# Strassen once more on a third of P4, two convolution steps on ScalarE and GpSimd, and S3 and S4 in other buffers

## The chip, the cores and the metric

One core of a Trainium2 chip. The time is the device time in microseconds (us) of one execution, the median of several. Engines: PE (TensorE), DVE (VectorE), ACT (ScalarE), POOL (GpSimd); SP only issues DMAs.

## The reference, cut

`x` is (8, 4096, 192) and `weight` (8, 7), float32; `w_in` is (192, 2048) and `w_out` (2048, 192).

```python
w = softmax(weight)                       # over the 7 taps, for each of 8 heads
x_unf = x_pad[:, idx, :].reshape(B, S, K, H, group)
y = np.einsum('hk,bskhg->bshg', w, x_unf) # causal convolution over the sequence
h = y.reshape(B * S, D) @ w_in
g = h * np.clip(h + 3.0, 0.0, 6.0) / 6.0
return g @ w_out
```

## The kernel before, in words

The 32768 tokens are cut into 32 blocks of 1024. Block 0 goes another way while the weights are prepared; blocks 1 to 31 run the same program: `first_layer(i)`, then `second_layer(i)`. Every engine works its instructions off in the order in which the code issues them, and the code writes that order out by hand.

**Convolution.** `conv_jobs` (L855) makes seven steps over y, 128 x 1536 numbers each: step 0 is a multiplication on ACT, steps 1 to 6 are multiply-and-add instructions on DVE that read x and y from SBUF. For block i + 2 the first three are placed in `second_layer(i)`; the other four lie in the next `first_layer` (ahead of chunk 0 and behind chunks 1, 5 and 9). `split_high` and `split_rest` then cut y into three parts `y_own`, one instruction on ACT and two on DVE, and `swap_parts` copies them, with the two halves of the partitions exchanged, into `y_other`: six DMAs on SP's queue.

**First layer.** There are 16 chunks. For chunk n, `begin(n)` issues 12 matmuls into one of four PSUM slots of two banks and a multiplication by 4097 on ACT; `end(n)` issues 6 more, then `relu` on ACT and `gate` on DVE (L306), which write g to SBUF and free the slot. PE runs two chunks ahead of the gates. Chunks 0 to 7 read `y_own` and chunks 8 to 15 `y_other`. A slot is taken from the head of `free_slots` and put back at its end.

**Second layer.** g is 2 x 2 parts A11, A12, A21, A22 (8 pieces of 128 x 512 each), and so is w_out. Strassen's scheme makes seven products P1 to P7 of the sums S1 to S4 and T1 to T4 (table `prod`). A product is 512 tokens by 96 columns in three column pieces q = 0, 1, 2 of 32. PE works with four column streams j = 0 to 3 side by side, each 32 columns wide. `plain` puts eight 512-column matmuls (2 units each) on a stream; `small` puts four 256-column matmuls (1 unit each) of a second Strassen step on one. Before, the third piece (q = 2) of P1 and of P5 is made by such a second step on stream 3, seven small products each in place of one plain one; the parts they need are `small_sums` (L565): of A11 on POOL into tile `s1` during the first layer, of S1 on DVE into A22's place. Each stream holds 82 units. `do(t, fn)` places work for the other engines at unit t; all events are then sorted by t and issued.

**Sums.** S3 = A11 - A21 has a buffer of its own: three of the four pairs of pieces are made on POOL during the first layer, the last on DVE. S1 = A21 + A22 lies in A21's place: two pairs by accumulating DMAs that POOL issues (L552), two by DVE. S2 (in A11's place) and S4 (in A12's) are made by DVE in the second layer, in halves of 128 x 2048.

**End of the block.** DVE adds the products, transposes them, and SP stores them. Two `finish` jobs for the second half of the columns are carried over into the next block's first layer, where they stand ahead of chunk 0's gate on DVE. The second layer uses three of the four PSUM slots, so the next `begin(0)` finds a free one at once.

Of the kernel before, what the change touches and what calls it, by code (L numbers as in the profile page):

```python
# [25 lines left out]
def kernel(  # L26
# [93 lines left out]
    w_s = cst.tile([P, 2, 4, NP // 2, QS], F32, name="w_s")  # L120
# [154 lines left out]
    S2, S1, S4 = A11, A21, A12  # L275
# [101 lines left out]
    def out_direct(i, work):  # L377

        parts = [(k, q) for k in range(G) for q in range(G * NQ)]
        for r in range(0, len(parts), 4):  # L380
# [14 lines left out]
            if r == 0:  # L395
                for u in work:
                    u()
# [3 lines left out]
            for j, (k, q) in enumerate(parts[r : r + 4]):  # L401
                store_rows(i, k, q, xt, j)

    def g_sums(engine, which, slots, width):

        forms = {
            3: (S3, A11, A21, ALU.subtract),
            2: (S2, S1, A11, ALU.subtract), 4: (S3, A12, S2, ALU.subtract),
        }
        for n in which:  # L410
            o, a, b, op = forms[n]
            for p in slots[::width]:
                r = slice(p, p + width)
                engine.tensor_tensor(out=o[:, r], in0=a[:, r], in1=b[:, r], op=op)  # L414
# [7 lines left out]
    def product(bank, j, n, q, ks=every, **tokens):  # L422
        x, w = prod[n]
        return mm(bank, j, S3 if n == 7 else x, w, q, ks, True, True, **tokens)
# [65 lines left out]
    y_own, y_other, pools, s1 = [], [None], [], []  # L490

    def swap_parts():
        y_other[0] = pools[0].tile([P, 3, K3, N], F32, name="y_other", tag="other")
        for n in range(3):
            swap(y_other[0][:, n], y_own[n])


    def first_layer(i, jobs):
# [6 lines left out]
        def mms(n, part, start=False, stop=False):  # L505
            group, c = divmod(n, NP)
            for s in range(K3):
                for k in range(2):
# [3 lines left out]
                        rhs=r32(y_other[0][r, part, s] if group else y_own[part][r, s]),  # L512
# [23 lines left out]
        for n in range(count):  # L536
# [7 lines left out]
            if n == 1:  # L544
                s1.append(ot.tile([P, NP, N], F32, name="s1", tag="shared")[:])
            if n < NP and n % 2:
                small_sums(s1[-1], A11, (1, 2, 3, 4), nc.gpsimd, every[n - 1 : n + 1])
            if n > NP and n % 2:
                pair = slice(n - NP - 1, n - NP + 1)
                g_sums(nc.gpsimd if n + 1 < count else nc.vector, (3,), range(NP)[pair], 2)  # L550
                if n + 3 < count:
                    nc.gpsimd.dma_start(out=S1[:, pair], in_=A22[:, pair], accum_op=ALU.add)  # L552
        for pair in (slice(NP - 2, NP), slice(NP - 4, NP - 2)):
# [21 lines left out]
    def small_weights(to, w):  # L575
# [4 lines left out]
        t1, t2, t3, t4 = (to[:, n] for n in range(4))  # L580
# [3 lines left out]
    def second_layer(i, between):  # L584
        last = i + 1 == NB
        ours = [free_slots.pop(0) for _ in range(3)]
        d, e, b, x_, a, c = (psum[:, 2 * n + k] for n in ours for k in range(2))
        s5 = A22
# [4 lines left out]
        B, C, V = (bank[rows(3)] for bank in (x_, d, b))  # L593
        A, E = e[rows(3)], a[rows(3)]
        first, second, third = rows(0), rows(1), rows(2)
        late = {}
# [17 lines left out]
        def plain(j, bank, n, q, chunks, start=False):  # L614
            x, w = prod[n]
            x = S3 if x is None else x
# [6 lines left out]
        def small(n, m_, out, start=False):  # L623

            x, w = prod[n]
            sums, ws = (s1[-1], w_s[:, 0]) if n == 1 else (s5, w_s[:, 1])
            x11, x12, x21, x22 = four_parts(x)
            z1, z2, z3, z4 = four_parts(sums)
# [3 lines left out]
            t1, t2, t3, t4 = (ws[:, k] for k in range(4))  # L632
            xm, wm = {
                1: (x11, b11), 2: (x12, b21), 3: (z4, b22), 4: (x22, t4),
                5: (z1, t1), 6: (z2, t2), 7: (z3, t3),
            }[m_]
            for u in range(NP // 2):
                put(3, 1, lambda u=u: matmul(
                    3, out[:, lo], wm[:, u], xm[:, u], start and u == 0
                ))  # L640

        def tiles():
            new_results()
            late.update(zip(("p7", "p5", "u3"), (results[0][m, n] for n in range(3))))

        for q in range(NQ):
            plain(q, d, 4, q, every, True)
            before = (1, 6, NP)[q]
            plain(q, c, 7, q, every[:before], True)
            plain(q, e, 1, 2, range(5 + q, 6 + q))  # L650
            do(clock[q], copy, out=e[rows(q + 1)] if q < 2 else p1[third], in_=e[rows(q)])
            plain(q, c, 7, q, every[before:])
            plain(q, a, 2, q, every[:6], True)
            plain(q, b, 6, q, every)
            plain(q, a, 2, q, every[6:])
            plain(q, b, 3, q, every)

        def level_two(n, p, chunks, order):
            chunks, first_fill = list(chunks), [True]

            def fill(k):
                plain(3, b, n, 2, [chunks.pop(0) for _ in range(k)], first_fill.pop() if first_fill else False)

            steps = {
                1: lambda: copy(out=B[:, lo], in_=A[:, lo]),
                2: lambda: copy(out=p()[first, lo], in_=A[:, lo]),
                6: lambda: copy(out=C[:, lo], in_=B[:, lo]),
                5: lambda: copy(out=p()[second, lo], in_=E[:, lo]),
                7: lambda: add(p()[second, hi], C[:, lo], p()[second, lo]),
                3: lambda: add(p()[second, lo], B[:, lo], p()[second, lo]),  # L670
                4: lambda: copy(out=p()[first, hi], in_=C[:, lo]),
            }
            to = {1: A, 2: A, 6: B, 5: E, 7: C, 3: B, 4: C}
            for step in order.split():
                if step[0] == "x":
                    fill(int(step[1]))
                else:
# [275 lines left out]
```

## Time and profile before

| | us |
|---|---|
| median of 3 runs | 2231.11 (2230.29 to 2231.27) |
| profiled execution, its own time | 2230.5 |
| its span, first to last instruction | 2228.4 |
| PE busy | 2219.4 (100%) |
| DVE busy | 1872.5 (84%) |
| ACT busy | 1390.0 (62%) |
| POOL busy | 827.7 (37%) |

The granted TensorE clock was 1.0 throughout. The page counts an instruction as busy from its recorded start to its end, so time in which it is held up inside counts too. In a timeline, a line gives the start in us, the length, engine, source line, operation, output and input, shapes, and in brackets how long the engine was idle before and what released it. L numbers are lines of the kernel before; PEld is the loading of weights, which runs ahead of the matmuls.

What the groups of the page give for the operations that the change touches (mean of one):

| operation | engine | ns |
|---|---|---|
| convolution step, 128 x 1536 (L861) | DVE | 1807 |
| multiplication of convolution step 0 (L859) | ACT | 1575 |
| S3 difference of a pair, 128 x 1024 (L414) | POOL | 3040 |
| the same | DVE | 1339 |
| small sum of a pair, 128 x 256 (L573) | POOL | 755 to 1095 |
| small sum of all pieces, 128 x 1024 (L573) | DVE | 1223 |
| half of S2 or S4, 128 x 2048 (L414) | DVE | 2284 |
| gate, 128 x 1024 (L306) | DVE | 1219 |
| addition, 96 x 512 (L458) | DVE | 668 to 689 |
| addition, 32 x 256 (L458) | DVE | 427 |

### The profile page before, as it was taken

To read this page: it belongs to the slowest core of one execution; us is meant where nothing else is said; L and a number is where in the kernel's file an instruction comes from. 1 tells how busy PE (TensorE), PEld (TensorE's weight loads), DVE (VectorE), ACT (ScalarE), POOL (GpSimd) and SP (SyncE) were. 2 spreads that over 40 slices of the span, in tenths; PEclk is the share of its full clock that TensorE was granted. 3 is DMA by queue.
4 is the path that set the end of the run, shared out by engine and by line. 5 is a ranking of instruction groups with operands and counts; after the bars stand their busy time and mean duration, and the time that the engine had idled before them with its cause. 6 is when DMAs were issued, how large, how long until landed. Compare 5 with 4: busy or idle time off the path is not lost.

```text
span 2228.4 us, 50173 instructions
## 1 busy us (share of the span) xinstructions
PE 2219.4 (100%) x21432; PEld 1528.0 (69%) x21432; DVE 1872.5 (84%) x1636; ACT 1390.0 (62%) x1676; POOL 827.7 (37%) x689
## 2 busy tenths in 40 slices
PE   9999999999999999999999999999999999999998
PEld 5467776677766777766777667776667776677765
DVE  8888888888888888888888888888888888888876
ACT  7467665576655676555776556665567665577653
POOL 2444432344422444223443234442244432344322
PEclk9999999999999999999999999999999999999999
DMA  6344224443244342344422443323444234443232
GB/s 157 69 84 86 48 59 91 84 84 62 54 82 91 78 80 46 71 91 84 84 50 56 91 89 79 71 48 79 91 81 85 48 61 91 84 84 59 52 72 34
DMA packets 254063, 166.57 MB, mean 75 GB/s; under 512 B 208528, under 2 KB 213648, under 8 KB 253840
## 3 DMA queue, kind: packets, MB, share of 16 engines
q1 hardware_dynamic: 235416, 129.53, 28.4%
q0 software_dynamic: 17184, 33.57, 8.7%
q8 instruction: 168, 2.75, 0.5%
q14 instruction: 55, 0.45, 0.1%
q10 hardware_dynamic: 1240, 0.27, 0.1%
HBM read 31.72 MB, written 25.17 MB: 26 GB/s over the span
## 4 chain that ended last, share of the span: by engine, by line
PE 100%; DVE 0%; issue 0%; ACT 0%; DVEq 0%
PE psum L609 49%; PE psum L510 46%; PE psum L296 2%; PE psum L341 2%; PE psum L755 0%; PE psum L763 0%; DVE results L458 0%; DVE results L464 0%; ACT results L709 0%; DVE zeros L111 0%; DVEq L464 0%; DVE x L96 0%; DVE half L233 0%; DVE bias_e L150 0%; DVE bias_e L149 0%
## 5 line engine op out<-in xcount | busy, mean ns | idle before, releaser
L609 PE MATMUL psum<-g,w_out 128*32 128x512 f32 (+1 forms) x6696 | 967.3, 553 | 0.0
L306 DVE SCALAR_TENSOR_TENSOR g<-g,psum 128x1024 f32<-128x1024 f32 (+1 forms) x528 | 618.1, 1186 | 228.2 <-ACT g L302 223.9
L573 POOL TENSOR_TENSOR s<-g 128x256 f32<-128x256 f32 x248 | 271.6, 1095 | 1232.3 <-DVE g L306 1232.3
L302 ACT ACTIVATE g<-psum,half 128x1024 f32<-128x1024 f32 (+1 forms) x528 | 565.1, 1089 | 0.8
L609 PEld LDWEIGHTS psum<-g,w_out 128*32 128x32 f32 x6696 | 368.9, 110 | 247.3 <-issue 127.4
L521 ACT ACTIVATE psum<-psum 128x1024 f32<-128x1024 f32 x496 | 500.2, 1008 | 57.7 <-PE psum L510 55.9
L510 PE MATMUL psum<-y,w_in 64*128 64x512 f32 x4464 | 521.7, 388 | 0.0
L510 PE MATMUL psum<-y_other,w_in 64*128 64x512 f32 x4464 | 517.0, 386 | 0.0
L510 PEld LDWEIGHTS psum<-y,w_in 64*128 64x128 f32 x4464 | 413.3, 184 | 116.1 <-issue 26.0
L510 PEld LDWEIGHTS psum<-y_other,w_in 64*128 64x128 f32 x4464 | 415.7, 184 | 91.0 <-ACT psum L521 5.1
L609 PE MATMUL psum<-s,w_out 128*32 128x512 f32 (+1 forms) x3224 | 465.3, 576 | 0.0
L861 DVE SCALAR_TENSOR_TENSOR y<-x,c_sb,y 128x1536 f32<-128x1536 f32 x186 | 336.1, 1807 | 1.3
L414 POOL TENSOR_TENSOR s<-g 128x1024 f32<-128x1024 f32 x93 | 282.7, 3040 | 30.2 <-DVE g L306 30.2
L609 PE MATMUL psum<-g,w_s 128*32 128x256 f32 x1240 | 282.8, 379 | 0.0
L609 PEld LDWEIGHTS psum<-s,w_out 128*32 128x32 f32 x3224 | 151.7, 110 | 81.7 <-issue 50.0
L609 PEld LDWEIGHTS psum<-g,w_s 128*32 128x32 f32 x1240 | 136.4, 110 | 68.4
L414 DVE TENSOR_TENSOR s<-g 128x2048 f32<-128x2048 f32 (+1 forms) x93 | 180.6, 1969 | 1.1
L609 PE MATMUL psum<-s,w_s 128*32 128x256 f32 x744 | 170.7, 379 | 0.0
L573 DVE TENSOR_TENSOR g<-g 128x1024 f32<-128x1024 f32 x124 | 151.7, 1223 | 5.2
L414 DVE TENSOR_TENSOR g<-g 128x2048 f32<-128x2048 f32 x62 | 139.1, 2284 | 0.0
L606 ACT COPY psum<-psum 32x512 f32<-32x512 f32 x93 | 51.3, 551 | 131.9 <-PE psum L609 131.9
L458 DVE TENSOR_TENSOR results<-psum,results 32x256 f32<-32x256 f32 (+1 forms) x125 | 68.0, 544 | 47.7 <-issue 46.3
(82 smaller groups left out, 1270.7 us busy)
## 6 DMA issues: line engine op xcount, KB each, us to landing
y_other<-y SPq DMA_DIRECT2D x186, 384.0 KB, 5.1
g<-g POOLq DMA_DIRECT2D x62, 512.0 KB, 5.0
out_dram<-results SPq DMA_DIRECT2D x378, 64.0 KB, 2.0
x<-in_x_dram SPq DMA_DIRECT2D x53, 388.5 KB, 7.7
stage<-in_moe_w_in_dram SPq DMA_DIRECT2D x16, 192.0 KB, 4.6
stage<-in_moe_w_out_dram SPq DMA_DIRECT2D x8, 384.0 KB, 5.6
x<-in_x_dram SPq DMA_DIRECT2D x7, 384.0 KB, 8.3
x<-in_x_dram POOLq DMA_DIRECT2D x2, 388.5 KB, 6.7
```

What stands on the lines that cost most here:

```text
L296: nc.tensor.matmul(out=psum[:, b], lhsT=w[r], rhs=src, start=start, stop=stop, skip_group_check=onto,)
L302: nc.scalar.activation(r6, h, ACT.Relu, bias=half[:], scale=1.0 / 6.0)
L306: nc.vector.scalar_tensor_tensor(out=g_, in0=g_, scalar=1.0, in1=h, op0=ALU.min, op1=ALU.mult)
L341: lambda p=p: nc.tensor.matmul(out=bank[j * QS : (j + 1) * QS, tokens], lhsT=w_out[:, p, w, cols], rhs=x[:, p, tokens], start=(first and p ...
L414: engine.tensor_tensor(out=o[:, r], in0=a[:, r], in1=b[:, r], op=op)
L458: nc.vector.tensor_tensor(out=out, in0=x, in1=y, op=op)
L510: nc.tensor.matmul(out=psum[:, 2 * slots[n] + k], lhsT=r32(w_in_parts[part][r, c, s]), rhs=r32(y_other[0][r, part, s] if group else y_own[ ...
L521: nc.scalar.mul(both(n), both(n), 4097.0)
L573: engine.tensor_tensor(out=o, in0=p, in1=q, op=op)
L606: streams[3].append((t - 0.5, lambda: fn(*args, **kw)))
L609: nc.tensor.matmul(out=out, lhsT=w, rhs=x, start=start, stop=True, tile_position=(0, j * QS), skip_group_check=True,)
L861: jobs.append(lambda k=k: nc.vector.scalar_tensor_tensor(out=y[:], in0=x[:, :, k : k + N], scalar=c_sb[:, k : k + 1], in1=y[:], op0=ALU.mu ...
```

## The change

P4's third column piece is now made by a second Strassen step too, as P1's and P5's are. Its seven small products take A22's small sums, which POOL makes during the first layer (four instructions for each of four pairs, as for A11), and three more small weight sums, which POOL makes once. All small products now lie on stream 3, and the plain pieces that were there lie on streams 0 to 2; P5's first small product is spread over all four streams. Each stream holds 81 units.

Convolution steps 1 and 2, placed in the second layer, are each one multiplication on ACT into A12's place and three additions of 128 x 512 on POOL, in place of one instruction on DVE. The other four stand behind chunks 1, 4, 7 and 9 of the first layer.

S3 lies where y_own was (the two share a buffer in turn); all four pairs are made on DVE, two of them behind chunks 11 and 14. S4 has the buffer in which A22's small sums were. S2 lies in A22's place and S1's small sums in A11's. `split_high`, `split_rest` and `swap_parts` move from units 13, 15 and 18 to units 37, 37 and 41, behind the load of x on SP's queue.

The second layer now takes all four PSUM slots and gives them back in the order (a, e), (b, x_), (f, h), (d, c). The products are added in another way: five additions of 96 x 512 and seven of 32 x 256 in the second layer, and three of 96 x 512 in the finish jobs. In block 0's part the swaps come behind two of the three groups of stores, and the third group is stored from ACT's queue.

```diff
-    w_s = cst.tile([P, 2, 4, NP // 2, QS], F32, name="w_s")
+    w_s = cst.tile([P, 3, 3, NP // 2, QS], F32, name="w_s")
...
-    S2, S1, S4 = A11, A21, A12
+    S2, S1 = A22, A21
...
+    early_pairs = {11: 0, 14: 2}
...
             if n < NP and n % 2:
-                small_sums(s1[-1], A11, (1, 2, 3, 4), nc.gpsimd, every[n - 1 : n + 1])
-            if n > NP and n % 2:
-                pair = slice(n - NP - 1, n - NP + 1)
-                g_sums(nc.gpsimd if n + 1 < count else nc.vector, (3,), range(NP)[pair], 2)
-                if n + 3 < count:
-                    nc.gpsimd.dma_start(out=S1[:, pair], in_=A22[:, pair], accum_op=ALU.add)
-        for pair in (slice(NP - 2, NP), slice(NP - 4, NP - 2)):
+                for k, x in ((1, A11), (4, A22))[: 1 if n > NP // 2 else 2]:
+                    small_sums(small_a[k], x, (1, 2, 3, 4), nc.gpsimd, every[n - 1 : n + 1])
+            if n == NP:
+                s3[0] = pools[1].tile([P, NP, N], F32, name="s3", tag="own")[:]
+            if n in early_pairs:
+                k = early_pairs[n]
+                pair = slice(k, k + 2)
+                g_sums(nc.vector, (3,), range(NP)[pair], 2)
+                nc.gpsimd.dma_start(out=S1[:, pair], in_=A22[:, pair], accum_op=ALU.add)
+                small_sums(small_a[4], A22, (1, 2, 3, 4), nc.gpsimd, every[k + 4 : k + 6])
+        for pair in (slice(4, 6), slice(6, 8)):
+            g_sums(nc.vector, (3,), range(NP)[pair], 2)
             add(S1[:, pair], A21[:, pair], A22[:, pair])
...
-        ours = [free_slots.pop(0) for _ in range(3)]
-        d, e, b, x_, a, c = (psum[:, 2 * n + k] for n in ours for k in range(2))
+        ours = [free_slots.pop(0) for _ in range(4)]
+        a, e, d, c, b, x_, f, h = (psum[:, 2 * n + k] for n in ours for k in range(2))
...
+        step(1, 5, 53.8)
+        for n, k in ((4, 1), (1, 1), (4, 2), (4, 4), (4, 6), (4, 5), (4, 7), (4, 3), (1, 6)):
+            step(n, k)
+        step(1, 2, 53.8)
+        step(5, 1)
+        step(1, 7, 54)
+        step(1, 3, 54.1)
+        for n, k in ((5, 2), (1, 4), (5, 6), (5, 5), (5, 7), (5, 3), (5, 4)):
+            step(n, k)
...
+        for t, n in ((21.1, 1), (21.1, 3), (45, 2), (62, 4)):
+            do(t, small_sums, small_a[5], S1, (n,), nc.vector)
+        do(20.6, g_sums, nc.vector, (2,), every, 4)
+        do(53.6, tiles)
...
+        do(55.4, g_sums, nc.vector, (4,), every[:4], 4)
+        do(55.5, g_sums, nc.vector, (4,), every[4:], 4)
+        do(63, lambda: add(p4[:], c[m], p4[:]))
+        do(64, lambda: add(late["u3"], a[m], late[1]))
+        do(64, lambda: store(i, late["u3"], 0, 0))
+        do(73.1, lambda: add(p4[:], p4[:], late[1]))
+        do(73.1, lambda: add(late["p7"], b[m], p4[:]))
+        do(73.1, lambda: store(i, late["p7"], 1, 0))
+        do(73.2, lambda: add(late["u2"], b[m], late[1]))
...
-        free_slots.extend(ours[n] for n in (0, 2, 1))
+        free_slots.extend(ours[n] for n in (0, 2, 3, 1))
...
-            jobs = {4 * n + 1: [job] for n, job in enumerate(conv[4:])}
-            jobs[-1] = left + conv[3:4]
+            jobs = {n: [job] for n, job in zip((1, 4, 7, 9), conv[3:])}
+            jobs[-1] = left
...
+            def sum_tap(k):
+                scaled = A12[:, 3 * (k - 1) : 3 * k]
+                return (
+                    lambda: nc.scalar.mul(scaled, x_tile[0][:, :, k : k + N], c_sb[:, k : k + 1]),
+                    *[
+                        lambda s=s: nc.gpsimd.tensor_tensor(
+                            out=y[:, s], in0=y[:, s], in1=scaled[:, s], op=ALU.add
+                        )
+                        for s in range(K3)
+                    ],
+                )
...
-                between = [(13, split_high), (15, split_rest), (18, swap_parts)]
+                between = [(36.6, new_own), (37, split_high), (37, split_rest), (41, swap_parts)]
             if i + 2 < NB:
-                between += [(20, begin_conv), (60, lambda: conv[0]()), (72, lambda: conv[1]()), (73, lambda: conv[2]())]
+                between += [(20, begin_conv), (56.4, lambda: conv[0]())]
+                for t, k in ((66, 1), (71, 2)):
+                    between += [(t, job) for job in sum_tap(k)]
```

## The prediction

> **What bounds the kernel now.** I read the page's busy shares and chain first, then the chain in order of time, the table by windows, and the timelines of VectorE (DVE), ScalarE (ACT) and GpSimd (POOL) for one block in the middle. Busy shares and chain, from the page:
>
> ```profile
> PE 2219.4 (100%) x21432; PEld 1528.0 (69%) x21432; DVE 1872.5 (84%) x1636; ACT 1390.0 (62%) x1676; POOL 827.7 (37%) x689
> ...
> PE psum L609 49%; PE psum L510 46%; PE psum L296 2%; PE psum L341 2%; PE psum L755 0%; PE psum L763 0%; DVE results L458 0%; DVE results L464 0%; ACT results L709 0%; DVE zeros L111 0%; DVEq L464 0%; DVE x L96 0%; DVE half L233 0%; DVE bias
> ```
>
> TensorE (PE) alone sets the end: 49% second layer (L609), 46% first layer (L510). The table by windows splits one of the 31 equal blocks (i = 1 to 31) at the start of its second layer; columns: window, its us, then busy us of PE, PEld, DVE, ACT, POOL:
>
> ```profile
> 989.85:1022.77 32.92, 32.92 (x292) 26.75 (x296) 25.12 (x21) 31.03 (x32) 21.97 (x20) 1.00 0.16 26
> 1022.77:1058.24 35.47, 35.47 (x387) 21.11 (x386) 32.80 (x28) 12.00 (x21) 3.58 (x2) 1.00 0.59 120
> ```
>
> A block is 32.92 + 35.47 = 68.39 us, all of it PE. But DVE is close behind in the second layer: 32.80 of 35.47. POOL is free there. The DVE timeline of that window, cut:
>
> ```profile
> 1022.82 3.48 DVE L306 SCALAR_TENSOR_TENSOR g<-g,psum 128x1024 f32<-128x1024 f32 x3 [2.18 <-ACT g L302]
> 1026.34 1.28 DVE L414 TENSOR_TENSOR s<-g 128x1024 f32<-128x1024 f32 x1
> 1027.65 2.36 DVE L458 TENSOR_TENSOR g<-g 128x1024 f32<-128x1024 f32 x2
> ...
> 1039.31 4.49 DVE L414 TENSOR_TENSOR g<-g 128x2048 f32<-128x2048 f32 x2
> 1043.71 4.49 DVE L414 TENSOR_TENSOR s<-g 128x2048 f32<-128x2048 f32 x2
> ...
> 1054.15 3.63 DVE L861 SCALAR_TENSOR_TENSOR y<-x,c_sb,y 128x1536 f32<-128x1536 f32 x2
> 1058.89 0.69 DVE L458 TENSOR_TENSOR results<-results 96x512 f32<-96x512 f32 x1 [1.11 <-ACT results L709]
> ```
>
> DVE idles only 1.53 us at 1048.2 and 1.11 us at the end. The third thing to see is what POOL and DVE do to each other. In the steady block POOL's first sum starts beside a convolution step (998.17 to 999.98 on DVE):
>
> ```profile
> 998.38 2.20 POOL L573 TENSOR_TENSOR s<-g 128x256 f32<-128x256 f32 x1 [40.24 <-DVE g L306]
> 1000.65 0.75 POOL L573 TENSOR_TENSOR s<-s,g 128x256 f32<-128x256 f32 x1
> ```
>
> It ends 0.6 us after the step; the next takes 0.75. The reverse shows once, in block 1, where POOL is late with other work (timeline of all engines, cut):
>
> ```profile
> 124.99 2.40 DVE L861 SCALAR_TENSOR_TENSOR y<-x,c_sb,y 128x1536 f32<-128x1536 f32 x1
> 125.04 0.74 POOL L573 TENSOR_TENSOR s<-g 128x256 f32<-128x256 f32 x1
> 125.74 2.26 POOL L573 TENSOR_TENSOR s<-g,s 128x256 f32<-128x256 f32 x1
> ...
> 128.58 1.00 PEld L510 LDWEIGHTS psum<-y_other,w_in 64*128 64x128 f32 x10 [0.46 <-DVE g L306]
> ```
>
> A step of 1.81 takes 2.40: it stood 0.6 us behind one POOL sum, the next POOL sum stood behind it, and PE then waited 0.46 us for the gate behind the step. The two engines take turns.
>
> **What the Trainium skill says.** "SBUF — State Buffer", section Who interferes with whom: a DVE instruction with two SBUF inputs and a GpSimd instruction that reads SBUF exclude each other for their whole length; a DVE instruction with one SBUF input doesn't. The trace agrees: 2.40 for 1.81 above, while the gates (one input in PSUM) keep 1.16 us spacing beside POOL at 1022.8. The same page, section SBUF: two separate sides, says that POOL-issued DMAs are held up by DVE's 2-port modes; none of that shows here (L552 takes 1.19 to 1.26 us). "Perfetto Trace Analysis", section GPSIMD Engine Instruction: use start-to-start spacing. So a 128x256 sum costs 0.70 (1000.65 to 1001.36), less than its 0.74.
>
> **The change, step by step.** Let T1 be the start of the second layer and T0 that of the next first layer.
>
> *PE.* The unit is a 256-column matmul, 35.47 / 82 = 0.433 us: each of the four column streams had 82 (0 to 2: 41 matmuls of 512 columns; stream 3: 56 small and 13 large). After, each has 81. Gain 0.43 us a block, 13.4 us over 31. Stream 3 is now small alone; small matmuls ran at 0.431 a unit against 0.429 for large ones, so at most 0.1 of it is lost; I keep 0.43. The second layer of PE alone is 35.04.
>
> *DVE, second layer, without POOL.* In the new order, priced by start-to-start spacing in the timeline: wait of the first gate 0.05; three gates 3 x 1.16 = 3.5; three S3 differences (one before; POOL did the others) 3 x 1.2 = 3.6; two S1 sums 2.3; S2 and S4, four halves of 2.2 = 8.8; four small sums 4 x 1.2 = 4.8; two halves of split_rest 3.3; seven 32x256 additions (four before) x 0.47 = 3.3; five 96x512 additions (three before) x 0.71 = 3.55; two transposes 1.45. Sum 34.65. Its last one, the addition of step (5,3), reads bank x_, and the additions of p7 and u2 just before it read b. The new second layer holds all four PSUM slots, and `begin(1)` of the next first layer takes slot (b, x_): PE gets there at T0 + 1.37 (12 of 288 matmuls: 32.92 / 24), that is T1 + 36.4, and needs the release some 0.1 earlier, 36.3. So without POOL, DVE is on time with 1.65 us to spare. Behind a waiting begin(1) stands every later matmul.
>
> *POOL against DVE.* POOL has 32 small sums a block (16 before), minus three S3 differences of 2.3, plus six 128x512 additions. The last are not in the trace: between 0.70 (256 columns) and 2.4 (1024), on the line through both 1.25. Its work is 32 x 0.70 + 6 x 1.25 + 2 DMAs x 0.8 = 31.5 us, which must fit beside DVE's two-input instructions. Pairs 1 and 3 now queue eight sums each, so POOL runs through the whole first layer. Its last four sums (A22, chunks 6 and 7) stand behind the accumulating DMA, which waits for the S3 difference on DVE at about T1 + 4; they start near T1 + 5. DVE then has four two-input instructions in a row (S3, S1, S3, S1), followed by S2, which overwrites A22 and so waits for those very sums. Taking turns: nothing for the first, 0.6 for each of the next three, 0.7 for S2 to wait out the last: 2.5 us. The S3 difference before them meets a POOL sum with about even odds: 0.3 of 0 to 0.6. The new addition p4 + late[1] (two SBUF inputs) meets the 1.25 us additions of the convolution: 0 to 1.2, I take 0.3. Sum 3.1, bounds 2.0 to 4.3. None can be negative, since a wait only adds.
>
> So DVE is done at 34.65 + 3.1 = T1 + 37.75, 1.45 after the 36.3 that PE allows: begin(1) stalls 1.45 us.
>
> *First layer.* It keeps four convolution steps on DVE (1.72 each; the one ahead of chunk 0 moves behind chunk 1), and gains one finish addition (0.7) and the two S3 differences at chunks 11 and 14. The gates wait for ACT anyway (2.04 us a chunk against 1.16). A step delays the next gate by 1.72 + 1.16 - 2.04 = 0.84, less than the spare: PE does not stall with steps at 1, 5, 9 now. With steps at 4, 7, 9 POOL is in mid run: each waits 0 to 0.6, and block 1 shows what 0.6 makes of it (0.46 us of PE's weight loads, which run ahead of the matmuls, so less of its time). After one stall the later ones are covered. I take 0.2 a block (0 to 0.8).
>
> *What costs nothing.* ACT's two multiplications (1.58 each) lie in the second layer, where ACT is busy 12 of 35.47. The POOL additions end near T0 + 4, the step that waits for them comes at T0 + 8.3. The six swaps (5.1 us to landing, 10.7 at most) move behind split_rest and past the x load on SP's queue, to about T1 + 25; with 6.5 us of issue and 10.7 they land by T0 + 7, and chunk 8 reads them at T0 + 16. S3 in y_own's place: y_own is rewritten at unit 37, P7's last read is unit 33. The DMA of pair 2 lands at T1 + 5.1 + 5.0 = 10.1 and is read at unit 24 = 10.4; its 7.0 maximum would cost 1.7. The T4 small weights add four POOL operations once (0.5 to 1.9 each): 0.3 us. The last block's finish has one more addition in each half: 0.8 us.
>
> *Sum.* A full block: -0.43 + 1.45 + 0.2 = +1.22 us. Blocks 1 to 29: +35.4. Block 30, without convolution additions: +0.9. Block 31, without split_rest: -0.4. Ends: +1.1. Together +37. The profiled execution of 2230.5 us (span 2228.4 and 2.1 around it; the median of the runs is 2231.1) becomes 2267.5; on the median, 2268.
>
> **The rivals.**
> *PE stays the bound (faster).* If the turns cost under 1.65 us, for instance because POOL's last sums fit under the gate of chunk 15 (1.16 us without a conflict) or DVE keeps the port, begin(1) never waits: -13.4 + 1.1 + 0 to 0.2 x 31, 2219 to 2225, say 2219. For it: PE waits for nothing now, and the margin is 2 us in 70. Against it: 2.5 us of turns in one place that no other work covers. It decides at 1.65 us.
> *POOL wins once more (slower still).* The first convolution addition becomes ready at about T1 + 30.5, within 0.3 us of DVE's fourth small sum. If POOL is first, that sum waits 1.1 more, and matmul (5,3) at unit 73 with it: 29 x 1.1 = 32, so 2300.
> *The stream gives nothing.* If 81 small units take as long as 82 mixed ones and DVE is in time, 2232.
>
> **How the numbers follow.** Forecast (DVE late at begin(1), 2240 to 2290) 0.57; PE stays the bound, 2219, 0.26; no change 0.07; POOL first, 2300, 0.10. What a measurement of this kernel can tell from no change is 0.2%, 4.5 us. Faster 0.26, same 0.07, slower 0.57 + 0.10 = 0.67. The range reaches down to the second case whole and to 2300: 2216 to 2300. The likeliest case alone: turns of 2.0 to 4.3 give 2230 to 2303, but only with all parts at one end, so 2240 to 2290.
>
> **What would show it.** PEld L510 waiting some 1.5 us in each block for DVE L459 (the additions); DVE busy over 90% of the span; S3 and S1 instructions of 1.2 us recorded at 1.8 between T1 + 5 and T1 + 12; POOL busy near 60%. If these have 1.2 us and PE's chain still shows two lines only, the forecast is wrong and the first rival right; if small matmuls wait for DVE L585, the second.

## The result, and the profile after

| | us |
|---|---|
| before, median of 4 runs | 2231.12 (2230.29 to 2231.27) |
| after, median of 4 runs | 2287.97 (2285.27 to 2288.7) |
| ratio | 1.0253, 95% interval 1.0236 to 1.0271 |
| profiled span, before and after | 2228.4 and 2286.0 |

The change costs 57 us. Busy shares and the first line of the chain, from the page of the kernel after:

```profile
PE 2261.7 (99%) x22176; PEld 1655.6 (72%) x22176; DVE 2123.8 (93%) x1858; ACT 1497.0 (65%) x1858; POOL 1368.7 (60%) x1270
...
PE 58%; DVE 22%; POOL 7%; DMA 5%; issue 5%; ACT 2%; SPq 1%; ACTq 0%; DVEq 0%; POOLq 0%
```

PE still reads 99% busy, since its record counts the time in which a matmul is held up. The chain tells more: PE held 100% of it before, and now holds 58%, while DVE, POOL and DMA hold 34% together. The end is no longer set by PE alone. The table by windows for one equal block (columns as before), cut at the start of its second layer:

```profile
1016.94:1051.08 34.14, 33.94 (x289) 26.89 (x288) 30.94 (x27) 30.79 (x32) 26.62 (x28) 1.00 0.22 43
1051.08:1087.14 36.06, 35.66 (x410) 23.52 (x408) 35.48 (x30) 15.88 (x27) 16.72 (x14) 1.00 0.50 101
```

34.14 + 36.06 = 70.20 us against 68.39. DVE is busy for 35.48 of the 36.06 us of the second layer (32.80 of 35.47 before). The DVE timeline of that layer, cut to the places that matter (T1 = 1051.08):

```profile
1056.08 1.41 DVE L415 TENSOR_TENSOR s<-g 128x1024 f32<-128x1024 f32 x1
1057.52 1.63 DVE L459 TENSOR_TENSOR g<-g 128x1024 f32<-128x1024 f32 x1
1059.08 1.75 DVE L415 TENSOR_TENSOR s<-g 128x1024 f32<-128x1024 f32 x1
1060.86 1.64 DVE L459 TENSOR_TENSOR g<-g 128x1024 f32<-128x1024 f32 x1
1062.45 2.79 DVE L415 TENSOR_TENSOR g<-g 128x2048 f32<-128x2048 f32 x1
...
1084.94 1.65 DVE L459 TENSOR_TENSOR p<-p,results 96x512 f32<-96x512 f32 x1
1086.62 0.69 DVE L459 TENSOR_TENSOR results<-psum,p 96x512 f32<-96x512 f32 x1
1087.34 0.71 DVE L465 STREAM_TRANSPOSE results<-results 96x512 f32<-96x512 f32 x1
1087.98 1.11 DVE L459 TENSOR_TENSOR results<-psum,results 96x512 f32<-96x512 f32 x2
1089.19 1.58 DVE L459 TENSOR_TENSOR results<-results 96x512 f32<-96x512 f32 x1
```

And POOL beside it:

```profile
1055.57 1.20 POOL L562 DMA_DIRECT2D g<-g  x1
1056.34 1.73 POOL L585 TENSOR_TENSOR s<-g 128x256 f32<-128x256 f32 x1
1058.14 1.60 POOL L585 TENSOR_TENSOR s<-s,g 128x256 f32<-128x256 f32 x1
1059.71 1.71 POOL L585 TENSOR_TENSOR s<-g 128x256 f32<-128x256 f32 x1
1061.38 1.71 POOL L585 TENSOR_TENSOR s<-g,s 128x256 f32<-128x256 f32 x1
...
1082.27 7.94 POOL L952 TENSOR_TENSOR y<-y,g 128x512 f32<-128x512 f32 x6 [19.18 <-ACT g L950]
```

The two lists interlock. POOL's sum (0.70 alone) is recorded at 1.6 to 1.7 and ends a little after a DVE instruction; DVE's S3 and S1 (1.22 alone) are recorded at 1.4 to 1.75, and the last three of the four end after a POOL sum (what lengthened the first is not shown); S2 (2.28 alone) starts with one POOL sum still to come and takes 2.79. At the end, p4 + late[1] (0.69 alone) stands 1.65 us beside POOL's convolution additions. PE then waits for DVE; its weight loads around the start of the next first layer, cut from the same block's timeline:

```profile
1087.14 1.23 PEld L516 LDWEIGHTS psum<-y_own,w_in 64*128 64x128 f32 x12 [0.41 <-issue]
1088.68 0.18 PEld L516 LDWEIGHTS psum<-y_own,w_in 64*128 64x128 f32 x1 [0.31 <-DVE results L459]
1089.14 3.04 PEld L516 LDWEIGHTS psum<-y_own,w_in 64*128 64x128 f32 x28 [0.28 <-DVE results L459]
```

Twelve loads for `begin(0)`, then two waits of `begin(1)`, for the additions that read bank b and then for the next one. All such waits of the run, from the view of waits (waiter <- releaser: us in all, times, longest):

```profile
POOL s L585 <- DMA out_dram<-results: 188.4, 26, 8.7
...
PEld psum L516 <- DVE results L459: 25.0, 58, 0.6
...
PEld psum L626 <- ACT psum L623: 16.5, 26, 1.2
PEld psum L516 <- DVE g L306: 15.3, 41, 0.5
PEld psum L626 <- DVE results L459: 13.6, 42, 0.8
```

**Where the 57 us are.** I take the start of each layer's first matmul from the trace, and the lag of later matmuls behind the pace of the kernel before (means of blocks 2 to 29).

| place | us each | x | us |
|---|---|---|---|
| block 1, first layer: 41.0 against 33.6 | +7.3 | 1 | 7.3 |
| first layers 34.16 against 32.92: `begin(1)` +0.67, gates +0.54 | +1.23 | 29 | 35.7 |
| second layers 35.91 against 35.47 | +0.44 | 29 | 12.8 |
| last block | +0.9 | 1 | 0.9 |

The sum is 56.7; the spans differ by 57.6. The second layer's +0.44 is a gain of 0.37 less waits of 0.81. The gain is seen in the last block of the last three kernels below: nothing in its second layer waits, and it takes 35.17 against 35.54 before (both to the end of the last matmul). Against that block, the fourth stream, stream 3, which ends last, is late by 0.81 in the mean, in two places:

- At T1 + 10.6, by 0.50. In most blocks it is 0.25: a small product of P5 that stands on the third stream waits for ACT's copy (L623) of the sum before it, and stream 3's next matmul starts late with it. In a third of the blocks it is up to 1.3, since the same product reads S1's second pair, whose accumulating DMA has not landed.
- At T1 + 25, by 0.30. The small product (1,4), the fourth of P1, writes a bank that DVE's addition of (1,7) must have read.

The last row of the waits has this second place, and another at T1 + 33.9, where (5,4) stands behind the addition of (5,7). There only the weight loads wait, some 0.3 us; no matmul of stream 3 is late by it. (The first row, POOL's wait of some 7 us for the tile of its sums to be stored, holds up none of PE's work in these blocks.)

Block 1 has a loss of its own. Its start in the timeline of all engines, cut:

```profile
100.84 3.65 ACTq L372 DMA_DIRECT2D out_dram<-results  x4
...
104.61 1.57 ACT L892 ACTIVATE y<-x,c_sb 128x1536 f32<-128x1536 f32 x1 [13.26 <-DMA out_dram<-results]
...
106.21 1.93 ACT L527 ACTIVATE psum<-psum 128x1024 f32<-128x1024 f32 x2
...
107.27 16.07 PE L516 MATMUL psum<-y_own,w_in 64*128 64x512 f32 x114 [4.30 <-ACT psum L527]
```

The third group of block 0's stores now sits on ACT's queue. It is ready only at 100.84, and its four DMAs take ACT 3.65 us to issue. Behind them stand a convolution step and the first multiplication by 4097, and PE waits 4.30 us for that. The pause costs more than itself. The windows behind it, columns as before and then the granted clock, the DMA share and GB/s:

```profile
107.27:113.39 6.12, 6.12 (x28) 4.76 (x30) 3.82 (x3) 3.51 (x4) 0.00 (x0) 0.50 0.98 241
113.39:119.00 5.61, 5.61 (x52) 5.09 (x50) 4.44 (x4) 5.04 (x6) 3.61 (x3) 1.00 0.01 2
```

For 6.12 us PE runs at half the clock: the three groups of 12 matmuls after the pause take 2.73, 2.56 and 1.75 us, where 1.36 is usual. So some 4.4 of the 7.3 us are the pause, and 3.0 are the clock. In all six kernels of this document that leave these stores on ACT's queue, PE pauses here for 4.7 to 6.1 us from matmul to matmul, and the clock reads 0.5 for 6.83 us (3.41 in one). In the kernel before and in the five that move the stores back there is no pause, and the clock stays at 1.0 here. Why the clock falls is not shown.

### The profile page after: what moved, and what is told of

It is laid out like the page before. It is cut to its first block, busy times and chain, and to the rows that moved or that the text cites. A ratio compares the mean times of both kernels' runs of the same rounds, so it can differ in the third digit from the quotient of the medians.

```text
span 2286.0 us, 52821 instructions
## 1 busy us (share of the span) xinstructions
PE 2261.7 (99%) x22176; PEld 1655.6 (72%) x22176; DVE 2123.8 (93%) x1858; ACT 1497.0 (65%) x1858; POOL 1368.7 (60%) x1270
## 4 chain that ended last, share of the span: by engine, by line
PE 58%; DVE 22%; POOL 7%; DMA 5%; issue 5%; ACT 2%; SPq 1%; ACTq 0%; DVEq 0%; POOLq 0%
PE psum L516 35%; PE psum L626 18%; POOL s L585 7%; DVE s L415 6%; DVE results L459 4%; DVE p L459 3%; DVE g L585 3%; DMA g<-g 2%; DMA y_other<-y_own 2%; PE psum L296 2%; PE psum L341 2%; DVE y_own L480 2%; DVE g L306 2%; DVE results L465 1%; DVE y_own L910 1%
## 5 line engine op out<-in xcount | busy, mean ns | idle before, releaser
L626 PE MATMUL psum<-g,w_out 128*32 128x512 f32 (+1 forms) x6448 | 823.4, 527 | 5.1 <-DMA g<-g 5.1
L585 POOL TENSOR_TENSOR s<-g 128x256 f32<-128x256 f32 x496 | 488.3, 984 | 251.3 <-DMA out_dram<-results 188.4
L626 PE MATMUL psum<-s,w_out 128*32 128x512 f32 (+1 forms) x3968 | 620.9, 539 | 0.0
L626 PEld LDWEIGHTS psum<-g,w_out 128*32 128x32 f32 x6448 | 414.1, 110 | 203.7 <-ACT psum L623 16.5
L952 POOL TENSOR_TENSOR y<-y,g 128x512 f32<-128x512 f32 x174 | 238.4, 1402 | 537.3 <-ACT g L950 537.3
L516 PE MATMUL psum<-y_own,w_in 64*128 64x512 f32 x4464 | 551.1, 392 | 8.9 <-DVE results L459 4.4
L516 PEld LDWEIGHTS psum<-y_own,w_in 64*128 64x128 f32 x4464 | 452.6, 185 | 101.3 <-DVE results L459 25.0
L415 DVE TENSOR_TENSOR s<-g 128x1024 f32<-128x1024 f32 x186 | 335.5, 1818 | 1.0
L585 POOL TENSOR_TENSOR s<-s,g 128x256 f32<-128x256 f32 x248 | 307.7, 1241 | 19.4
L626 PEld LDWEIGHTS psum<-s,w_out 128*32 128x32 f32 x3968 | 273.0, 109 | 59.9 <-issue 1.7
L626 PE MATMUL psum<-g,w_s 128*32 128x256 f32 x1240 | 283.5, 380 | 0.0
L585 POOL TENSOR_TENSOR s<-g,s 128x256 f32<-128x256 f32 x248 | 279.7, 1128 | 0.0
L626 PE MATMUL psum<-s,w_s 128*32 128x256 f32 x992 | 236.8, 381 | 0.0
L626 PEld LDWEIGHTS psum<-g,w_s 128*32 128x32 f32 x1240 | 132.6, 110 | 85.4 <-DVE results L459 13.6
L585 DVE TENSOR_TENSOR g<-g 128x1024 f32<-128x1024 f32 x124 | 148.7, 1220 | 1.2
```

The costliest lines, as they stand in the source:

```text
L516: nc.tensor.matmul(out=psum[:, 2 * slots[n] + k], lhsT=r32(w_in_parts[part][r, c, s]), rhs=r32(y_other[0][r, part, s] if group else y_own[ ...
L585: engine.tensor_tensor(out=o, in0=p, in1=q, op=op)
L626: nc.tensor.matmul(out=out, lhsT=w, rhs=x, start=start, stop=True, tile_position=(0, j * QS), skip_group_check=True,)
L952: lambda s=s: nc.gpsimd.tensor_tensor(out=y[:, s], in0=y[:, s], in1=scaled[:, s], op=ALU.add)
```

## The experiments

My theory after the result: the loss of a block is DVE's second-layer list, lengthened by turns with POOL's small sums and convolution additions, and PE waits for it in a few places; block 1 is a separate loss by the store queue. The main rivals: PE's own new order is slower, or the waits for S1's DMA and the banks' order cost the time whatever POOL does. Ratios are against the kernel before, with 95% intervals. Layer times are means of blocks 2 to 29, to be read against 32.92 and 35.47 before, 34.16 and 35.91 after.

**Stores of block 0 back on SP.**

```diff
-                store_rows(i, k, q, xt, j, (nc.sync, nc.scalar)[r // 8])
+                store_rows(i, k, q, xt, j)
```

> Block 0's third group of stores goes back from ACT's queue to SP's; nothing else changes. Theory: the 7.3 us that block 1's first layer lost come from ACT, which issues four stores (3.65 us) ahead of y's scaling and of the first multiplications by 4097; then the time falls by 6 to 7 us, to about 2281. Rival: the late swaps or the longer list of small weights on GpSimd hold block 1; then it stays at 2288.

Measured: 2284.34 us, 1.0238 (1.0221 to 1.0255): 3.6 us less, where 6 to 7 were expected. Block 1's first layer is mended (33.56), but its second takes 41.88, so block 1 as a whole gets back only 0.9 us; most of the rest lies in the later first layers (34.07 against 34.16), for a reason that is not shown. In the chain around that place of this kernel:

```profile
140.51 4.88 POOL s L585 x3
145.39 5.04 DMA g<-g
150.43 0.14 issue
150.56 1.49 PE psum L626 x8
```

POOL's small sums begin at 115.19, since their tile is in part still being stored (4.36 us of wait for the stores to land), so the accumulating DMA behind them is issued late, and PE waits for it. The loss was moved from ACT's queue to POOL's, not removed.

**All stores on SP, and the swaps behind them.**

```diff
-                store_rows(i, k, q, xt, j, (nc.sync, nc.scalar)[r // 8])
-            if r == 4:
+                store_rows(i, k, q, xt, j)
+            if r == 8:
                 work[1]()
```

> Block 0's stores all on SP's queue, the six swaps behind them. With the third group on SP but behind the swaps, block 1's first layer was back at 33.6 us and its second layer took 41.9 in place of 35.4: GpSimd began its sums at 115.2, when the stores that free the tile had landed. Theory: with the stores ahead of the swaps GpSimd starts some 4 us earlier and this wait falls from 6.5 to about 3: 2281. Rival: GpSimd's own work in block 1 is the limit: 2284, no better; or the swaps land too late for chunk 8: above 2284.

Measured: 2279.24, 1.0216 (1.0201 to 1.0231). Block 1 is 33.48 + 36.77 where the kernel after has 41.0 + 35.37: 6.1 us of it, and 8.7 us less in all. This was the first kernel that got back most of what block 1 had lost.

**Slots given back in another order,** so that `begin(1)` doesn't take the bank pair that DVE reads last.

```diff
-        free_slots.extend(ours[n] for n in (0, 2, 3, 1))
+        free_slots.extend(ours[n] for n in (0, 3, 2, 1))
```

> The four PSUM slots are given back in the order (a, e), (f, h), (b, x_), (d, c), so that begin(1) takes (f, h), which no late VectorE addition reads. Theory: begin(1) waits 0.67 us a block for the additions of p7, u2 and step (5,3) and for nothing else; then this wait goes, but some 0.3 of it comes back at begin(3) and begin(4), since VectorE is as late as before: 2272 to 2280. Rival: the wait at begin(1) is a wait for VectorE as a whole, and moves on unshortened to the next gate: 2286 to 2290.

Measured: 2278.29, 1.0209 (1.0194 to 1.0224). `begin(1)` waits no more, but 0.54 of its 0.67 us comes back at `begin(3)` and `begin(4)`, behind the same additions and the first gates. The wait is only the place where DVE's lateness is met, not its cause.

**Small sums that only write.** The 32 small sums a block on POOL become fills with zeros of the same size: their arithmetic is left out, and with it the reading of SBUF. The Trainium skill ("SBUF — State Buffer", section Who interferes with whom) says that a GpSimd instruction that only writes doesn't contend with DVE's two-input instructions.

```diff
-            engine.tensor_tensor(out=o, in0=p, in1=q, op=op)
+            if engine is nc.gpsimd:
+                engine.memset(o, 0.0)
+            else:
+                engine.tensor_tensor(out=o, in0=p, in1=q, op=op)
```

> Leaves out the arithmetic of the small sums on GpSimd: each of the 32 instructions a block only writes zeros to the same place, so that none reads SBUF; VectorE's list and every order stay. Theory[...]: VectorE's S3, S1 and S2 instructions and convolution steps go back to 1.2, 1.2, 2.28 and 1.81 us, about 3.6 us a block less, the gate, begin(1) and (5,4) waits go, TensorE is the bound: 2225 to 2232. Rival: VectorE's longer list alone, or GpSimd's lateness, is the cause: within 10 us of 2288 for the list, and the instructions keep 1.6 us.

Measured: 2236.27, 1.0023 (1.0015 to 1.0031): 51.7 of the 56.9 us are gone. Layers 32.96 and 35.38; only block 1 keeps its loss (40.5). The groups of the kernel after, shapes kept apart (count | busy us, mean ns | idle before):

```profile
L894 DVE SCALAR_TENSOR_TENSOR y<-x,c_sb,y 128x1536 f32<-128x1536 f32 x128 | 259.9, 2031 | 5.6 <-ACT y L892 5.4
L415 DVE TENSOR_TENSOR s<-g 128x1024 f32<-128x1024 f32 x124 | 196.2, 1582 | 0.0
...
L459 DVE TENSOR_TENSOR g<-g 128x1024 f32<-128x1024 f32 x62 | 101.6, 1638 | 2.1
...
L459 DVE TENSOR_TENSOR p<-p,results 96x512 f32<-96x512 f32 x31 | 48.7, 1570 | 1.0
```

and of this kernel:

```profile
L897 DVE SCALAR_TENSOR_TENSOR y<-x,c_sb,y 128x1536 f32<-128x1536 f32 x128 | 232.0, 1812 | 5.9 <-ACT y L895 5.6
L415 DVE TENSOR_TENSOR s<-g 128x1024 f32<-128x1024 f32 x124 | 151.1, 1219 | 0.0
...
L459 DVE TENSOR_TENSOR g<-g 128x1024 f32<-128x1024 f32 x62 | 76.0, 1225 | 2.1
...
L459 DVE TENSOR_TENSOR p<-p,results 96x512 f32<-96x512 f32 x31 | 22.0, 709 | 1.0
```

In order: convolution step, S3, S1, p4 + late[1]. All are back at their lengths of before, as the skill's sentence has it. (The fills also spare POOL time, which is busy for 27% of the span in place of 60%; that the DVE instructions themselves get shorter speaks for the reading.) p4 + late[1] is back although the convolution additions still read: in three blocks that I read, it starts 0.1 us ahead of one of them here, and the addition takes 1.7 us in place of 1.3; in the kernel after, it starts 0.2 us behind one and is itself the one that waits. So POOL's small sums, by what they do to DVE, are the cause of nearly all of the loss; how much of it is their reading and how much the time that the shorter fills spare POOL is not separated.

The second layer is 35.38 here, only 0.09 us less than before, though no matmul waits for DVE in it. What is left is the copy. Two rows of this kernel's waits:

```profile
DVE results L459 <- ACT results L704: 44.6, 31, 2.7
...
PEld psum L629 <- ACT psum L626: 17.5, 31, 1.1
```

The second row (L626 here is L623 of the kernel after) is the wait at T1 + 10.6, in all 31 blocks; it makes stream 3 late by 0.25 in nearly all of them, 0.28 in the mean. No POOL work stands in it: the new order of PE and ACT brought it, and in the last three kernels, where that product stands four units later, it is gone. The first row is a wait of DVE that matters further below.

**Convolution additions that only write.** The six additions a block become fills; their arithmetic is left out.

```diff
-                        lambda s=s: nc.gpsimd.tensor_tensor(
-                            out=y[:, s], in0=y[:, s], in1=scaled[:, s], op=ALU.add
-                        )
+                        lambda s=s: nc.gpsimd.memset(y[:, s], 0.0)
```

> Leaves out the arithmetic of the convolution additions on GpSimd: each of the six a block only writes zeros to y. Theory (turns): the addition p4 + late[1] and the first one of the finish go from 1.55 to 0.69 us, begin(1) waits no longer, the wait of (5,4) for (5,7) stays: 2288 - 29 x 0.67 = 2269. Rival: these two additions are not on the path, or begin(1) waits for the work before them: 2283 to 2289.

Measured: 2257.09, 1.0118 (1.0103 to 1.0133): 30.9 us less, where I had expected about 19. The two additions beside them fall from 1570 and 1543 to 689 and 687 ns; S3 and S1 keep 1587 and 1638. `begin(1)` waits no more and the gates' lag falls from 0.54 to 0.32, since the first gates come earlier. So the additions, six instructions, cost more than half of the loss, because they meet DVE at the one point after which PE waits. The parts overlap (51.7 + 30.9 is more than 56.9): either alone puts DVE back ahead of `begin(1)`.

**Convolution steps 1 and 2 back on DVE.**

```diff
-                for t, k in ((66, 1), (71, 2)):
-                    between += [(t, job) for job in sum_tap(k)]
+                between += [(72, lambda: conv[1]()), (73, lambda: conv[2]())]
```

> Undoes one part: convolution steps 1 and 2 go back to VectorE at units 72 and 73, as in the kernel before; the rest of the change stays. Theory: on GpSimd they cost VectorE two waits of 0.86 us, on VectorE 3.44 us, of which 2.6 more lie ahead of p7 and u2, so begin(1) waits 2.6 longer in 29 blocks: about 2360. Rival: the additions on GpSimd are the harm and VectorE has room: 2257 (what the run without their reads took) to 2290.

Measured: 2354.59, 1.0553 (1.0538 to 1.0569). The convolution additions are no mistake in themselves: without them DVE has 3.6 us more to do, and the block takes 72.40. Moving the two steps away from DVE is worth more than the turns that they bring.

**DVE's tail in another order.** p4 + late[1] stands right behind the fourth small sum, ahead of POOL's first addition; (5,7) comes ahead of u3; ACT's first multiplication comes later.

```diff
+        do(62.1, lambda: add(p4[:], p4[:], late[1]))
         do(63, lambda: add(p4[:], c[m], p4[:]))
-        do(64, lambda: add(late["u3"], a[m], late[1]))
...
-        do(73.1, lambda: add(p4[:], p4[:], late[1]))
+        do(73.05, lambda: add(late["u3"], a[m], late[1]))
...
-                for t, k in ((66, 1), (71, 2)):
+                for t, k in ((69.6, 1), (71, 2)):
```

> Only the order at the end of the second layer: the addition p4 + late[1] right behind VectorE's fourth small sum, ahead of GpSimd's first convolution addition, whose multiplication on ScalarE moves behind the copy of (5,5); the addition of (5,7) ahead of u3 and its transpose. Theory: p4 + late[1] is back at 0.71 us, (5,4) no longer waits (0.43 a block) and begin(1) little (0.67 now): 2250 to 2260. Rival: these waits only show that VectorE's list is too long, and come back at the next gates: 2275 or more.

Measured: 2260.6, 1.0132 (1.0117 to 1.0147), just above what I expected. p4 + late[1] is back at 681 ns, and `begin(1)` does not wait. The whole arithmetic is kept, and nearly half of the loss goes with this order (27.4 of 56.9 us). Left are the gates (0.37), the second layer (35.80) and block 1.

**All mends together, and the convolution steps in thirds:** both orders above, S1's second pair read four units later, swaps last, and the four steps of the first layer cut into twelve of 128 x 512, so that no gate stands behind more than one short instruction.

```diff
-            jobs = {n: [job] for n, job in zip((1, 4, 7, 9), conv[3:])}
+                pieces_ = [job for k in range(3, KC) for job in tap_thirds(conv_x[0], k)]
+                for n, job in zip((1, 1, 2, 3, 4, 5, 6, 7, 8, 9, 10, 12), pieces_):
+                    jobs.setdefault(n, []).append(job)
...
-        plain(2, c, 7, 2, every[:4])
+        plain(2, c, 7, 2, every[:6])
```

> All of it together: PSUM slots given back in the order (a, e), (f, h), (b, x_), (d, c); the end of the second layer reordered; P5's small product of chunk 2 at unit 28 instead of 24; the convolution steps on VectorE in thirds of 128x512 between the gates; block 0's stores ahead of the swaps. Theory: each wait named so far is mended and no other comes up: a block of 68.4 to 68.7 us, block 1 some 4 us longer, 2236 to 2246. As the second layer of TensorE alone took 35.38 us without any wait (35.47 before), nothing under 2229 can come of it. Rival: with the longer list VectorE is late wherever it is put: above 2255.

Measured: 2255.15, 1.0112 (1.0095 to 1.0129); expected 2236 to 2246, so a miss. The first layer is mended (33.01), but the second is 36.01, with a new lag of 0.65 at units 9 to 18. The chain of this kernel at such a place:

```profile
957.98 1.13 POOL s L585
959.10 9.62 DMA g<-g
968.73 0.04 issue
968.77 3.23 PE psum L626 x18
```

The accumulating DMA, 5.0 us in the kernel after, takes 9.62 here. SP's timeline of the same stretch shows what else began:

```profile
958.63 0.58 SPq L82 DMA_DIRECT2D x<-in_x_dram  x1
959.26 0.61 SPq L83 DMA_DIRECT2D x<-in_x_dram  x1
```

The load of the next x, 777 KB in two DMAs, waits for the last convolution step to have read the old one. In the kernel after that is at 1044.8 (T0 + 27.9), 5.7 us ahead of the DMA; the last third, behind chunk 12, moves it to 0.5 us ahead. (In the next block, which doesn't wait, the load starts 0.66 us behind the DMA.) Two more kernels test that.

**The same without the thirds.**

```diff
-                for n, job in zip((1, 1, 2, 3, 4, 5, 6, 7, 8, 9, 10, 12), pieces_):
-                    jobs.setdefault(n, []).append(job)
+            jobs = {n: [job] for n, job in zip((1, 4, 7, 9), conv[3:])}
```

> All mends of the previous combined kernel but the thirds: slot order, tail order, pair 2 four units later, swaps last; the four convolution steps are whole again, at chunks 1, 4, 7, 9. Theory for the wait of that kernel (12 of its 31 blocks wait up to 2.6 us for the accumulating DMA, which then takes 9.6 us from issue to landing against 5.0): its last third, at chunk 12, keeps the x tile until T0 + 32.1, so the load of the next x (777 KB) starts within half a microsecond of the first accumulating DMA and shares the DMA engines with it; with whole steps that load starts near T0 + 28 and is done before. Then here: landing 5.0 to 7.0, no wait at units 9 to 18, second layer 35.4 to 35.5, first layer 33.2 to 33.4, time 2244 to 2250. Rival: the late landing comes with the earlier sums and the new order of reads (slots, tail, pair 2), not with the thirds: the wait stays, second layer near 36.0, time 2258 to 2265.

**The same with the thirds done by chunk 9.**

```diff
-                for n, job in zip((1, 1, 2, 3, 4, 5, 6, 7, 8, 9, 10, 12), pieces_):
+                for n, job in zip((1, 2, 3, 3, 4, 5, 5, 6, 7, 7, 8, 9), pieces_):
```

> All mends and the thirds, but the twelve thirds are done by chunk 9 instead of chunk 12 (three chunks take two of them). If the load of x is what the accumulating DMA meets, it now starts near T0 + 26 and is out of the way: landing 5.0 to 7.0, no wait at units 9 to 18, second layer 35.4, first layer 33.0 to 33.3, time 2237 to 2246. If the thirds themselves (eight more DVE instructions that meet GpSimd) make the DMA late, the wait stays and the time is 2250 to 2260.

Measured: 2252.93, 1.0098 (1.0083 to 1.0113), and 2287.06, 1.0251 (1.0234 to 1.0268). In both the DMA lands in a median of 5.0 and 5.1 us again (at most 6.9) and PE's lag at unit 18 is 0.02, so the load of x was what the DMA had met. This agrees with the Trainium skill ("SBUF — State Buffer", section "Can I just issue two DMAs to hit both halves?"), which says that all DMAs land on the same 16 engines. But both times missed. Without thirds the first layer is 33.34 as expected, while the second stays at 35.81: nothing is left at T1 + 10.6, but PE now reaches (1,4) earlier and waits 0.70 there for DVE's addition of (1,7), against 0.30 in the kernel after. With early thirds the second layer is 35.45 as expected (0.35 of it the wait of (1,4)) and the first takes 34.84: behind chunks 3, 5 and 7 stand two thirds, which take 1.94 to 2.40 us with POOL's turns in them, more than a whole step. PE's weight loads in one block of this kernel:

```profile
1034.91 3.99 PEld L516 LDWEIGHTS psum<-y_other,w_in 64*128 64x128 f32 x36 [0.99 <-DVE g L306]
1039.73 8.03 PEld L516 LDWEIGHTS psum<-y_other,w_in 64*128 64x128 f32 x72 [0.83 <-DVE g L306]
```

In these places each cut gives POOL one more turn. No kernel here beats the one before; the best with the whole arithmetic is 22 us behind it.

## Why the prediction was right, and where its sizes were off

It forecast +37 us by one mechanism, and +57 came by that mechanism and a start that I had priced wrongly.

*Turns between DVE and POOL: right, and shown.* The four instructions in a row at T1 + 5, S2 behind POOL's last sum, and p4 + late[1] beside the convolution additions are all in the timeline, and go when POOL only writes. POOL's last sums start at T1 + 5.26 (I had said near T1 + 5). The turns add up to 3.3 us as means of blocks 2 to 29, where I had 3.1, but they lie elsewhere: the S3 ahead of the row lost 0.3 as forecast, the row at T1 + 5 lost 0.2, 0.4, 0.6 and 0.4 us and S2 0.4, 2.0 in all where I had 2.5; p4 + late[1] lost 0.9 in every block where I had taken 0.3 as a mean of 0 to 1.2. POOL's wave starts at T1 + 30.8 to 31.5 in all blocks, and that addition at T1 + 33.8 to 34.4, so they meet in the same way each time, and a mean over chances was the wrong form for it.

*DVE's end: the right number by luck.* The additions that free the slot of `begin(1)` end at 1089.09, T1 + 38.0 (38.1 in the mean), against my 37.75. Two errors cancel in that. In the kernel with fills, where this row has no turn, DVE's list ends at T1 + 36.2 and not at 34.65: my sum of instructions left out a wait of 1.4 us for ACT's copy of (1,5) (the first row of that kernel's waits, 44.6 / 31), although the timeline before has an idle stretch of 1.53 ahead of such an addition. `begin(1)` is reached at T1 + 36.75 there, so the spare without turns is some 0.5 us and not 1.65. In the kernel after, DVE comes to that place later and no longer waits, so about 1.3 of the 3.3 us of turns cost nothing there, and the end moves by 2.0 instead of 3.1.

*`begin(1)`: the right wait, a smaller stall.* 1.45 us forecast, 0.67 measured. DVE's end was right as a number; PE itself came later than I had it. In the example block `begin(1)` is reached at T1 + 37.4, not 36.4.

*PE's gain: there, but eaten by waits.* I kept 0.43; without any wait the new streams gain 0.37 (35.17 against 35.54), so "at most 0.1 of it is lost" held. The step that failed is the one behind it: "the second layer of PE alone is 35.04" has no wait inside, and I listed only waits that I called free. Three cost: P5's small product behind ACT's copy 0.25, not listed; the second pair's DMA 0.25 in the mean, called free with a margin of 0.3 us (10.1 against 10.4); and (1,4) behind (1,7) 0.30, not listed. All lie ahead of `begin(1)`, and they moved the time little: while DVE's end sets the start of `begin(1)`, a slower PE only waits less there. PE's gain and the wait together were to give -0.43 + 1.45 = +1.02; the second layer and `begin(1)` together measured 0.44 + 0.67 = +1.11.

*Gates in the first layer: 0.2 forecast, 0.54 measured,* within the bound of 0 to 0.8 that I gave. A convolution step takes 2.03 us in the mean instead of 1.81, and the lag comes behind the steps: 0.3 behind that at chunk 4, 0.1 behind each of those at 7 and 9. My reason for the small value, that one stall covers the later ones, did not hold. The difference of 0.34 over 29 blocks is 10 us.

*The start: 0.3 forecast, 7.3 measured.* I priced the added weight sums on POOL and looked past the third group of stores, which the diff moves to ACT's queue. The step that failed is the one that counts every instruction on each queue it is moved to: four DMAs there took 3.65 us of ACT, with the first layer's first multiplication behind them. PE's pause made 4.4 us of the loss, and the half clock after it 3.0.

Together: 37, and 0.09 a block for the second layer with `begin(1)`, 0.34 for the gates and 7 for the start: 37 + 29 x 0.09 + 29 x 0.34 + 7 = 56.5, against 56.9 measured.

*The rivals.* "PE stays the bound" (2219) falls on DVE, which was not in time. Without the turns the time would be some 2229 (my estimate: 2236.27 less the 6.9 us that block 1 still loses there). With the copy's wait gone too, 0.25 x 31 = 8 us, the estimate would lie in this rival's range; that kernel was not built. "POOL first" is not seen: DVE's small sums keep 1220 ns, and no matmul waits for them. "The stream gives nothing" (2232) was wrong on both: the stream gains 0.37, and DVE was late. Of my signs, DVE over 90% (93), POOL near 60% (60) and S3 and S1 longer (1.58 and 1.64, not 1.8) were seen; the wait of PE's loads at `begin(1)` is 25.0 / 31 = 0.8 us, half of what I had named. One end of my likeliest range was uneven: turns of 2.0 alone give 2236, and 2230 only with no stall at the gates as well, while 2303 leaves their upper bound out.

*Still open:* what decides which of DVE and POOL goes first when both have work queued (at p4 + late[1] it was the one that had started first), and why the granted clock falls around the pause in block 1.

## What to carry to other kernels

Work moved to an idle engine is not free if the two must take turns, as DVE's two-input instructions and POOL's reads of SBUF did here: add up, place by place, which two-input instructions will stand beside which reads of POOL, and ask what waits at the end of that row. A wait that is removed by another order of slots, a cut into pieces or an earlier buffer comes back where the same late engine, or the transfer it has released, is met next; so price the engine's end, not the wait, and put the engine's own idle stretches into that sum. When work is saved on an engine, ask of each bank and copy in its new order what it will wait for; and read the diff for each DMA that changes its queue.

## What the runs showed of the hardware

- POOL's fills of the same tiles, which write SBUF and read nothing, left DVE's two-input instructions at their own length: S3 1219 ns, against 1582 beside sums.
- Four store DMAs of 64 KB took ACT's queue 3.65 us to issue, and SP's queue 7.59 us for twelve.
- An accumulating DMA of 512 KB lands in 5.0 us in the median, and took 9.62 us when a load of 777 KB had begun 0.5 us earlier.
- A DVE convolution step of 128 x 512 takes 0.74 us alone, but two in a row between POOL sums took 1.94 to 2.40.
- With a DVE addition and a POOL addition that both read SBUF, the later one waited: p4 + late[1] took 0.71 us when it started 0.1 us ahead of a POOL addition (which then took 1.7), and 1.63 when it started 0.2 us behind one.
- Around a pause of PE of 4.7 to 6.1 us in block 1, the granted clock fell to 0.5 in all six kernels that had the pause, for 6.83 us in five and 3.41 in one; in the six without it, it was 1.0 there.
